# Softplus taken from ScalarE's own table, in layer 0 and in the attention's exponentials

## The chip, the cores and the metric

The kernel runs on one core of one Trainium2 chip. The metric is device time in microseconds for one execution: lower is better. One core has a matrix engine (PE, with its weight loads shown apart as PEld), a vector engine (DVE), a scalar engine that evaluates activation functions (ACT), a general engine (POOL, hardly used here), and the queue that issues most DMA transfers (SP). Each engine runs its own instructions strictly in the order in which the program lists them, and waits for the others by semaphores.

## The reference

Three stages, one after the other, on 4 x 576 = 2304 tokens of width 512 (8 heads of 64):

```python
# 1. attention with a window of 64 positions
scores = scale * q @ k^T                      # scale = 1/8
scores = where(0 <= i - j < 64, scores, -1e9)
scores = scores - max(scores)
attn   = exp(scores); attn = attn / (sum(attn) + 1e-9)
x      = attn @ v                             # back to 2304 x 512
# 2. layer 0: 512 -> 2048 -> 512, activation softplus
h = x @ w_in
g = maximum(h, 0) + log1p(exp(-abs(h)))
x = g @ w_out
# 3. layer 1: the same shapes, activation: h >= 1: h; h <= -1: 0; else (h + 1)^2 / 4
```

All arrays are float32.

## The kernel before

**Layers.** Each layer goes over five blocks of tokens (four of 512 and one of 256). Within a block, a step takes one slice of 128 of the 2048 hidden units (two slices in the block of 256 tokens): `g1` makes the hidden values `h` of the slice in a PSUM bank (there are two such banks), then the activation is made by ACT and DVE, and two steps later (`LAG = 2`) `g2` multiplies it by the second weight matrix and adds it up in four PSUM banks `y`. The PE's order in a step is thus: the products for `h` of this step, then the products for `y` of the step two before.

**Precision.** Most products are made in a reduced format from two parts of each operand, a high part and the rest (`xh`, `xl`; `wh`, `wl`; `gh`, `gl`), as three matmuls for one product. Only the second product of layer 0's first block takes whole float32 operands (`g`, `wo`); the page counts each of those matmuls as two.

**The first block** of layer 0 is special, since everything starts there: its first four slices are worked on in two halves of 256 tokens, so that products can start as soon as the first half's attention is done. The later slices take all 512 tokens at once. While it runs, the weights arrive: each slice comes as two transfers of 512 KB (`raw`, three buffers, from the tensor shown as in_w), and each is decoded by one ACT operation (line 123) and three DVE operations (lines 124 to 126) into `bits` (the first matrix) or `wo` (the second). `halves` then makes `wh` (ACT, line 133) and `wl` (DVE, line 134). For `bits` that is needed at once; for `wo` the parts are needed from the second block on, and the queue of DVE has them wherever the scheduler put them.

**The attention** goes in units of 128 tokens, each of four parts: twice `sub_scores` (for the heads' even and odd halves), `sub_transpose` and `sub_pv`. Scores (PE, line 220) are copied (ACT), masked and their maximum taken (DVE, lines 251 to 253), exponentials made with their sums (ACT, line 257, four operations of 64 columns each time), divided (DVE, lines 261 to 263); the result `p` is transposed (PE, line 273), masked out of PSUM (DVE, line 286, into `pt`), multiplied by v (PE, line 305) and split into `xh` and `xl` (ACT line 312, DVE line 315). The attention of a block is spread over the steps of the block before it.

**The order** of all instructions on each engine is settled when the program is built: a scheduler with priorities places them by its own estimates, and the hardware then keeps that order.

**Layer 0's activation before** is the function `softplus`: ACT makes |h| out of PSUM, then exp(-|h|) = e, then (in the first block) u = 1 + e, and log(u); DVE makes u in the other blocks, then u - 1 - e, subtracts it from the logarithm as a correction, and adds max(h, 0), again out of PSUM. From the second block on, the helper `parts` then makes `gh` (ACT) and `gl` (DVE). Layer 1's `quadratic` uses `parts` as well and is not touched.

Of the kernel before, what the change touches and what calls it, by code (L numbers as in the profile page):

```python
# [1 line left out]

# [6 lines left out]
F32 = mybir.dt.float32  # L9
F32R = mybir.dt.float32r  # L10
I32 = mybir.dt.int32
AF = mybir.ActivationFunctionType
ALU = mybir.AluOpType
# [4 lines left out]
P = 128  # L18
# [4 lines left out]
NF = DFF // P  # L23
SCALE = 1.0 / D ** 0.5
MASKED = -1e9 / SCALE
EPS = 1e-9
LAG = 2
AHEAD = 1

# [10 lines left out]
def tile_window_attention_two_ffn(  # L40
# [10 lines left out]
    V, A, T = nc.vector, nc.scalar, nc.tensor  # L51
# [5 lines left out]
    gpool = ctx.enter_context(tc.tile_pool(name="g", bufs=3))  # L57
    tpool = ctx.enter_context(tc.tile_pool(name="tmp", bufs=2))
# [1 line left out]
    psum = ctx.enter_context(tc.tile_pool(name="psum", bufs=1, space=bass.MemoryType.PSUM))  # L60
    dpool = ctx.enter_context(tc.tile_pool(name="dram", bufs=1, space=bass.MemoryType.DRAM))

    A.preload_act_table_set("natural_log_exp_and_others")


    ident = cpool.tile([P, P], F32, name="ident")
# [27 lines left out]
    def pt(tag):  # L94
        return psum.tile([P, 512], F32, tag=tag, name=tag, bufs={"y": 4, "h": 2, "a": 2}[tag])
# [55 lines left out]
    sub_dve = {}  # L151
# [59 lines left out]
    def score_products(dbl, bank):  # L211
        banks = [pt(bank).rearrange("p (a s j) -> p a s j", a=2, s=2) for _ in range(2)]
        for s in range(2):
            qt, kt = qks.pop(2 * dbl + s)
            lo = 0 if (2 * dbl + s) % NCB else CB
            for a2 in range(2):
                for par in range(2):
                    for u in range(2):
                        a, r, o = 2 * a2 + par, slice(u * CB, (u + 1) * CB), slice(par * CB, (par + 1) * CB)
                        T.matmul(banks[u][o, a2, s, lo:], qt[r, a, r], kt[r, a, -(2 * CB - lo):],  # L220
                                 start=True, stop=True)
        return banks
# [3 lines left out]
    def sub_scores(dbl, u, bank):  # L226
        if u == 0:
            p2s[dbl] = apool.tile([P, NP, 2, CB], F32, tag="p2", name="p2")
        pr = p2s[dbl][:, 2 * u:2 * u + 2]
        sel = pr.rearrange("p a s j -> p (a s) j")  # L230
        mx = apool.tile([P, NP], F32, tag="mx", name="mx")
        sm = apool.tile([P, NP], F32, tag="sm", name="sm")

        def pe():
            if u == 0:
                scs[dbl] = score_products(dbl, bank)

        def a1():
            sc = scs[dbl][u]
            first = [s for s in range(2) if (2 * dbl + s) % NCB == 0]  # L240
            for s in first:
                V.memset(pr[:, :, s, :], MASKED)
            if first:
                s = 1 - first[0]
                A.copy(pr[:, :, s, :], sc[:, :, s, 0:CB])
            else:
                A.copy(pr, sc[:, :, :, 0:CB])

        def d1():
            sc = scs[dbl][u].rearrange("p a s j -> p (a s) j")  # L250
            V.copy_predicated(sel, msel.rearrange("p (o j) -> p o j", o=1).to_broadcast([P, NP, CB]), sc[:, :, CB:])
            V.tensor_reduce(mx, sel, axis=AX.X, op=ALU.max)
            sub_dve[dbl, u] = V.tensor_scalar_mul(mx, mx, -SCALE).ins  # L253

        def a2():
            for i in range(NP):
                A.activation(sel[:, i, :], sel[:, i, :], AF.Exp, bias=mx[:, i:i + 1], scale=SCALE,  # L257
                             accum_out=sm[:, i:i + 1])

        def d2():  # L260
            V.tensor_scalar_add(sm, sm, EPS)
            V.reciprocal(sm, sm)
            V.tensor_tensor(sel, sel, sm.rearrange("p (a o) -> p a o", o=1).to_broadcast([P, NP, CB]), op=ALU.mult)

        return pe, a1, d1, a2, d2

    def sub_transpose(dbl, bank):
# [102 lines left out]
    def parts(e, n):  # L370
        gh = gpool.tile([P, 512], F32R, tag="gh", name="gh")[:, :n]
        gl = gpool.tile([P, 512], F32R, tag="gl", name="gl")[:, :n]
        A.copy(gh, e)  # L373
        V.tensor_tensor(gl, e, gh.bitcast(F32), op=ALU.subtract)  # L374
        return gh, gl

    def softplus(h, n, split):

        e = tpool.tile([P, 512], F32, tag="e", name="e")[:, :n]
        u = tpool.tile([P, 512], F32, tag="u", name="u", bufs=1)[:, :n]  # L380
        l = tpool.tile([P, 512], F32, tag="l", name="l", bufs=1)[:, :n]
        g = e if split else gpool.tile([P, 512], F32, tag="gl", name="g")[:, :n]
        A.activation(e, h, AF.Abs)
        A.activation(e, e, AF.Exp, scale=-1.0)
        if not split:
            A.activation(u, e, AF.Copy, bias=1.0)
        else:
            V.tensor_scalar_add(u, e, 1.0)
        A.activation(l, u, AF.Ln)
        V.scalar_tensor_tensor(e, u, 1.0, e, op0=ALU.subtract, op1=ALU.subtract)  # L390
        V.tensor_tensor(l, l, e, op=ALU.subtract)  # L391
        V.scalar_tensor_tensor(g, h, 0.0, l, op0=ALU.max, op1=ALU.add)  # L392
        return parts(g, n) if split else (g,)

    def quadratic(h, n, split):

# [79 lines left out]
    for layer, i, f, kf, c0, n in steps:  # L476
# [33 lines left out]
        h = pt("h")[:, :kf * n]  # L510
        for j in range(kf):
            g1(layer, f + j, c0, n, *xs[layer, i], h[:, j * n:(j + 1) * n])
        if len(pend) >= LAG:
            emit_g2(pend.pop(0))
        g = (softplus, quadratic)[layer](h, kf * n, (layer, i) != (0, 0))
        pend.append((layer, i, f, kf, c0, n, g))
    while pend:
# [38 lines left out]
```

## Time and profile before

| | before |
|---|---|
| time, median of 3 runs | 908.78 us (906.93 to 909.26) |
| the profiled execution: its own time | 910.36 us |
| the profiled execution: span of the trace | 908.6 us |
| PE busy | 876.2 us (96% of the span) |
| PEld busy | 713.6 us (79%) |
| DVE busy | 621.7 us (68%) |
| ACT busy | 425.8 us (47%) |
| mean granted clock of TensorE | 0.996 of full speed |

The span is what the trace covers, from the first to the last instruction; the execution's own time is some 1.7 us more. Busy shares are means over the whole span; matmuls are pipelined and their ends are modelled, so that a busy PE may still have short holes. Times in the rows below are microseconds from the start of the span unless they say ns.

### The profile page before, as it was taken

Reading aid. Unit: us, or ns where it says so; the run is one execution under the profiler, and the core shown is the slowest. Engines: PE = TensorE matmul, PEld = TensorE weight load, DVE = VectorE, ACT = ScalarE, POOL = GpSimd, SP = SyncE. Lnnn points to the kernel's source line nnn. Section 1 sums busy time; section 2 is a strip of 40 time slices with the busy share of each in tenths; the row PEclk is TensorE's granted clock in tenths of the full one; section 3 lists DMA queues with packets and bytes.
Section 4 is the critical chain, followed back from the end, with each engine's and each line's share of the span. In section 5 each row is a group of like instructions: output and inputs, shape, how many; then the busy total and the mean of one; then the engine's idle time right before and its main releaser. Section 6 shows DMA issues by size and latency. Waiting matters only on the chain.

```text
span 908.6 us, 13022 instructions
## 1 busy us (share of the span) xinstructions
PE 876.2 (96%) x4984; PEld 713.6 (79%) x4984; DVE 621.7 (68%) x1166; ACT 425.8 (47%) x958; POOL 1.5 (0%) x10
## 2 busy tenths in 40 slices
PE   3889999899999999999999999999999999999998
PEld 2677656699888888888888888888888888888897
DVE  5899899797777787777999799854335333533342
ACT  5577684555455555554766455432223222322221
POOL 0000000000000000000000000000000000000000
PEclk9999999999999999999999999999999999999999
DMA  8474642334211231200632254120002000200010
GB/s 282 164 217 144 226 155 70 117 82 117 81 41 54 71 116 48 70 1 28 211 110 93 83 195 147 62 93 0 1 1 94 1 0 1 70 1 0 1 48 23
DMA packets 45374, 75.42 MB, mean 83 GB/s; under 512 B 4864, under 2 KB 21760, under 8 KB 45312
## 3 DMA queue, kind: packets, MB, share of 16 engines
q1 hardware_dynamic: 42912, 70.01, 23.9%
q10 hardware_dynamic: 2400, 4.59, 1.4%
q8 instruction: 39, 0.64, 0.3%
q14 instruction: 23, 0.19, 0.1%
HBM read 65.14 MB, written 9.44 MB: 82 GB/s over the span
## 4 chain that ended last, share of the span: by engine, by line
PE 83%; DVE 8%; DMA 3%; ACT 3%; issue 2%; SPq 0%; ACTq 0%; DVEq 0%
PE h L345 40%; PE y L365 22%; PE y L357 17%; DMA raw<-in_w 3%; PE a L305 2%; PE a L220 2%; DVE wl L134 1%; ACT p L257 1%; DVE pt L286 1%; PE a L273 1%; DVE l L391 1%; DVE e L390 1%; DVE wo L126 1%; DVE bits L125 1%; DVE g L392 1%
## 5 line engine op out<-in xcount | busy, mean ns | idle before, releaser
L345 PE MATMUL h<-xh,wh 128*128 128x512 f32 (+1 forms) x656 | 246.7, 376 | 4.5 <-DVE g L392 1.6
L345 PE MATMUL h<-xl,wh 128*128 128x512 f32 (+1 forms) x656 | 240.8, 367 | 0.5 <-DVE xl L315 0.3
L345 PE MATMUL h<-xh,wl 128*128 128x512 f32 (+1 forms) x656 | 240.6, 367 | 0.1
L345 PEld LDWEIGHTS h<-xh,wh 128*128 128x128 f32 x656 | 125.2, 191 | 30.0 <-ACT wh L133 3.7
L345 PEld LDWEIGHTS h<-xh,wl 128*128 128x128 f32 x656 | 125.3, 191 | 20.6 <-issue 0.3
L345 PEld LDWEIGHTS h<-xl,wh 128*128 128x128 f32 x656 | 125.2, 191 | 20.4 <-DVE xl L315 0.9
L373 ACT CAST gh<-e 128x512 fp32r<-128x512 f32 x128 | 79.4, 620 | 115.9 <-DVE e L392 68.5
L399 ACT ACTIVATE e<-e 128x512 f32<-128x512 f32 x72 | 45.5, 632 | 187.0 <-DVE e L398 186.9
L374 DVE TENSOR_TENSOR gl<-e,gh 128x512 fp32r<-128x512 f32 x128 | 88.3, 690 | 55.2 <-ACT gh L373 53.2
L398 DVE TENSOR_SCALAR e<-h 128x512 f32<-128x512 f32 x72 | 49.7, 690 | 104.1 <-PE h L345 104.1
L365 PE MATMUL y<-wh,gh 128*128 128x512 f32 x288 | 112.1, 389 | 0.0
L365 PE MATMUL y<-wl,gh 128*128 128x512 f32 x288 | 112.1, 389 | 0.0
L365 PE MATMUL y<-wh,gl 128*128 128x512 f32 x288 | 112.0, 389 | 0.0
L357 PE MATMUL y<-gh,wl 128*128 128x512 f32 (+1 forms) x256 | 93.2, 364 | 0.0
L357 PE MATMUL y<-gl,wh 128*128 128x512 f32 (+1 forms) x256 | 92.8, 362 | 0.0
L357 PE MATMUL y<-gh,wh 128*128 128x512 f32 (+1 forms) x256 | 92.8, 362 | 0.0
L400 DVE TENSOR_TENSOR e<-h,e 128x512 f32<-128x512 f32 x72 | 49.7, 690 | 41.0 <-ACT e L399 40.5
L365 PEld LDWEIGHTS y<-wh,gl 128*128 128x128 f32 x288 | 54.0, 188 | 11.3
L365 PEld LDWEIGHTS y<-wh,gh 128*128 128x128 f32 x288 | 54.1, 188 | 11.1
L365 PEld LDWEIGHTS y<-wl,gh 128*128 128x128 f32 x288 | 54.1, 188 | 10.8
L357 PE MATMUL y<-g,wo 128*128 128x512 f32 (+1 forms) x160 | 59.5, 514 | 0.0
L257 ACT ACTIVATE p<-p,mx 128x64 f32<-128x64 f32 x144 | 48.2, 336 | 23.7 <-DVE mx L253 23.6
(78 smaller groups left out, 1076.3 us busy)
## 6 DMA issues: line engine op xcount, KB each, us to landing
raw<-in_w SPq DMA_DIRECT2D x64, 512.0 KB, 3.9
qt<-in_q SPq DMA_DIRECT2D x34, 256.0 KB, 3.9
vt<-in_v SPq DMA_DIRECT2D x31, 256.0 KB, 2.9
kt<-in_k SPq DMA_DIRECT2D x29, 256.0 KB, 4.0
vt<-x2d SPq DMA_DIRECT2D x16, 256.0 KB, 5.4
x2d<-o SPq DMA_DIRECT2D x5, 512.0 KB, 2.9
out<-o SPq DMA_DIRECT2D x5, 512.0 KB, 3.1
x2d<-o ACTq DMA_DIRECT2D x4, 512.0 KB, 4.7
```

The source lines that it names most:

```text
L125: V.scalar_tensor_tensor(t, hi, -2 ** 31, t, op0=ALU.bitwise_and, op1=ALU.bitwise_or)
L220: T.matmul(banks[u][o, a2, s, lo:], qt[r, a, r], kt[r, a, -(2 * CB - lo):], start=True, stop=True)
L257: A.activation(sel[:, i, :], sel[:, i, :], AF.Exp, bias=mx[:, i:i + 1], scale=SCALE, accum_out=sm[:, i:i + 1])
L305: T.matmul(po[hf * CB:(hf + 1) * CB, a, s, :], vts[s][r, hd:hd + D], pp[s][r, 2 * hf + a // 2, a % 2, :], start=True, stop=True)
L345: T.matmul(h, w, x, start=i == 0, stop=i == len(ops) - 1)
L357: T.matmul(y[m][:, c0:c0 + n], w, x, start=f + i + c0 == 0, stop=f == NF - 1 and i == len(ops) - 1)
L365: T.matmul(y[t], l, r, start=f == 0 and i == 0, stop=f == NF - 1 and i == 2)
L373: A.copy(gh, e)
L374: V.tensor_tensor(gl, e, gh.bitcast(F32), op=ALU.subtract)
L398: V.tensor_scalar(e, h, -1.0, 1.0, op0=ALU.max, op1=ALU.min)
L399: A.activation(e, e, AF.Square, bias=0.5, scale=0.5)
L400: V.tensor_tensor(e, h, e, op=ALU.max)
```

## The change

Layer 0's activation is made by ACT's function Softplus, straight from the PSUM bank. In the first block, one ACT operation writes `g`, and DVE has nothing to do. In the other blocks, ACT evaluates Softplus twice from the same bank, once into `gh` (the reduced format) and once into `e` (float32), and DVE subtracts the two to get `gl`.

The attention's exponentials use the same function, so that one activation table serves the whole kernel: for a very negative argument softplus(t) is nearly exp(t), so softplus(s - 18) is nearly exp(s) times a constant, which the division by the sum cancels. The 18 goes into the bias (line 253's operation takes a second scalar), and the 1e-9 of the division is scaled to match. The number and shapes of these operations stay as they are.

```diff
--- before.py
+++ after.py
@@ -1,3 +1,4 @@
+import math
 from contextlib import ExitStack
 
 import concourse.bass as bass
@@ -23,7 +24,9 @@
 NF = DFF // P
 SCALE = 1.0 / D ** 0.5
 MASKED = -1e9 / SCALE
-EPS = 1e-9
+
+DOWN = 18.0
+EPS = 1e-9 * math.exp(-DOWN)
 LAG = 2
 AHEAD = 1
 
@@ -60,7 +63,7 @@
     psum = ctx.enter_context(tc.tile_pool(name="psum", bufs=1, space=bass.MemoryType.PSUM))
     dpool = ctx.enter_context(tc.tile_pool(name="dram", bufs=1, space=bass.MemoryType.DRAM))
 
-    A.preload_act_table_set("natural_log_exp_and_others")
+    A.preload_act_table_set("softplus")
 
 
     ident = cpool.tile([P, P], F32, name="ident")
@@ -250,11 +253,11 @@
             sc = scs[dbl][u].rearrange("p a s j -> p (a s) j")
             V.copy_predicated(sel, msel.rearrange("p (o j) -> p o j", o=1).to_broadcast([P, NP, CB]), sc[:, :, CB:])
             V.tensor_reduce(mx, sel, axis=AX.X, op=ALU.max)
-            sub_dve[dbl, u] = V.tensor_scalar_mul(mx, mx, -SCALE).ins
+            sub_dve[dbl, u] = V.tensor_scalar(mx, mx, -SCALE, -DOWN, op0=ALU.mult, op1=ALU.add).ins
 
         def a2():
             for i in range(NP):
-                A.activation(sel[:, i, :], sel[:, i, :], AF.Exp, bias=mx[:, i:i + 1], scale=SCALE,
+                A.activation(sel[:, i, :], sel[:, i, :], AF.Softplus, bias=mx[:, i:i + 1], scale=SCALE,
                              accum_out=sm[:, i:i + 1])
 
         def d2():
@@ -376,21 +379,17 @@
 
     def softplus(h, n, split):
 
+        if not split:
+            g = gpool.tile([P, 512], F32, tag="gl", name="g")[:, :n]
+            A.activation(g, h, AF.Softplus)
+            return (g,)
         e = tpool.tile([P, 512], F32, tag="e", name="e")[:, :n]
-        u = tpool.tile([P, 512], F32, tag="u", name="u", bufs=1)[:, :n]
-        l = tpool.tile([P, 512], F32, tag="l", name="l", bufs=1)[:, :n]
-        g = e if split else gpool.tile([P, 512], F32, tag="gl", name="g")[:, :n]
-        A.activation(e, h, AF.Abs)
-        A.activation(e, e, AF.Exp, scale=-1.0)
-        if not split:
-            A.activation(u, e, AF.Copy, bias=1.0)
-        else:
-            V.tensor_scalar_add(u, e, 1.0)
-        A.activation(l, u, AF.Ln)
-        V.scalar_tensor_tensor(e, u, 1.0, e, op0=ALU.subtract, op1=ALU.subtract)
-        V.tensor_tensor(l, l, e, op=ALU.subtract)
-        V.scalar_tensor_tensor(g, h, 0.0, l, op0=ALU.max, op1=ALU.add)
-        return parts(g, n) if split else (g,)
+        gh = gpool.tile([P, 512], F32R, tag="gh", name="gh")[:, :n]
+        gl = gpool.tile([P, 512], F32R, tag="gl", name="gl")[:, :n]
+        A.activation(gh, h, AF.Softplus)
+        A.activation(e, h, AF.Softplus)
+        V.tensor_tensor(gl, e, gh.bitcast(F32), op=ALU.subtract)
+        return gh, gl
 
     def quadratic(h, n, split):
 
```

Counted over the built programs, ACT goes from 826 to 654 instructions as the order lists them and DVE from 1168 to 884, PE keeps its 4330, and both versions have one ACT_TABLE_LOAD, at the start. Since the scheduler places instructions by its own estimates, the order changes too, in the first third of the program. Lines of the changed program stand three lower up to the activation (line 133 becomes 136).

**First place: ACT, about 31 us into the trace of before**, from the attention's exponentials `p_296` on (`g` is the activation, `h` its PSUM bank). Before:

```order
L257 ACTIVATE p_296,sm<-p_296,mx 128x64 x8
L383 ACTIVATE e<-h 128x256
L133 CAST wh_1542<-wo 128x512
L384 ACTIVATE e<-e 128x256
L123 ACTIVATE wo<-raw 128x512
L386 ACTIVATE u<-e 128x256
L133 CAST wh_450<-bits 128x512
L389 ACTIVATE l<-u 128x256
L383 ACTIVATE e<-h 128x256
L123 ACTIVATE bits<-raw 128x512
```

The changed program, from the same operation on:

```order
L260 ACTIVATE p_296,sm<-p_296,mx 128x64 x8
L384 ACTIVATE g<-h 128x256
L136 CAST wh_1362<-wo 128x512
L126 ACTIVATE wo<-raw 128x512
L136 CAST wh_441<-bits 128x512
L384 ACTIVATE g<-h 128x256
L126 ACTIVATE bits<-raw 128x512
L384 ACTIVATE g<-h 128x256
L126 ACTIVATE wo<-raw 128x512
L315 CAST xh<-a 128x4x128
L136 CAST wh_1435<-wo 128x512
```

Where the first activation took four operations with other work between them, it takes one, and two more activations and the next decodes (lines 123 and 126 of the two programs) have moved up behind it.

**Second place: DVE, at the border of the first and the second block**, about 152 us into the trace of before: the splits of `wo` (line 134, now 137) and the maximum of the scores `p_1485`, in the changed program `p_1305`. Before:

```order
L315 TENSOR_TENSOR xl<-a,xh 128x4x128
L134 TENSOR_TENSOR wl_1969<-wo,wh_1968 128x512
L134 TENSOR_TENSOR wl_1973<-wo,wh_1972 128x512
L134 TENSOR_TENSOR wl_2074<-wo,wh_2073 128x512
L134 TENSOR_TENSOR wl_2078<-wo,wh_2077 128x512
L134 TENSOR_TENSOR wl_2200<-wo,wh_2199 128x512
L390 SCALAR_TENSOR_TENSOR e<-u,e 128x512
L134 TENSOR_TENSOR wl_2204<-wo,wh_2203 128x512
L391 TENSOR_TENSOR l<-l,e 128x512
L134 TENSOR_TENSOR wl_2304<-wo,wh_2303 128x512
L392 SCALAR_TENSOR_TENSOR g<-h,l 128x512
L251 COPY_PREDICATED p_1485<-msel,a 128x256 x2
```

The changed program, up to the same operation (`pt` is the masked transpose of the unit before):

```order
L289 TENSOR_TENSOR pt_1185<-a,mown 64x512
L289 TENSOR_TENSOR pt_1185<-a,mprev 64x512
L289 TENSOR_TENSOR pt_1186<-a,mown 64x512
L289 TENSOR_TENSOR pt_1186<-a,mprev 64x512
L137 TENSOR_TENSOR wl_1972<-wo,wh_1971 128x512
L137 TENSOR_TENSOR wl_1976<-wo,wh_1975 128x512
L318 TENSOR_TENSOR xl<-a,xh 128x4x128
L137 TENSOR_TENSOR wl_2068<-wo,wh_2067 128x512
L254 COPY_PREDICATED p_1305<-msel,a 128x256 x2
```

Between `xl` and the masked copy of the scores stood seven splits and three operations of the activation; now one split stands there.

## Rows read from the trace of the kernel before

**Rows 1.** The page, busy tenths of PE in 40 equal slices.

```profile
PE   3889999899999999999999999999999999999998
```

**Rows 2.** Busy time by stretch: length, then PE, PEld, DVE, ACT, POOL (instructions), clock, DMA.

```profile
37.75:74.31 36.56, 30.50 (x258) 25.15 (x257) 33.50 (x84) 25.38 (x81) 0.00 (x0) 0.95 0.60 187
74.31:152.83 78.52, 77.16 (x376) 49.17 (x375) 73.38 (x135) 55.62 (x109) 0.00 (x0) 1.00 0.43 142
152.83:174.15 21.32, 17.82 (x137) 12.37 (x133) 18.11 (x38) 9.21 (x28) 0.00 (x0) 0.92 0.30 97
174.15:250.00 75.85, 75.30 (x699) 67.98 (x700) 59.63 (x130) 41.69 (x128) 0.00 (x0) 1.00 0.36 106
250.00:425.00 175.00, 175.00 (x1128) 142.03 (x1128) 133.23 (x260) 93.77 (x242) 0.00 (x0) 1.00 0.17 52
425.00:908.60 483.60, 479.40 (x2204) 400.27 (x2202) 278.82 (x454) 180.79 (x302) 0.00 (x0) 1.00 0.18 59
```

**Rows 3.** Waits of PE, 31.5 to 74.4 us: total us, times, longest.

```profile
PE a L305 <- DVE pt L286: 2.4, 2, 1.8
PE h L345 <- DVE g L392: 1.6, 2, 0.9
PE h L345 <- ACT wh L133: 0.9, 1, 0.9
```

**Rows 4.** Waits of PE, 74.4 to 250 us, the same columns.

```profile
PE a L273 <- DVE p L263: 3.9, 3, 2.6
PE h L345 <- DVE sm L262: 1.3, 1, 1.3
```

**Rows 5.** Timeline of PE, single rows: start, us, instruction [idle before].

```profile
60.79 0.28 PE L345 MATMUL h<-xh,wh 128*128 128x256 f32 x1
60.91 0.28 PE L345 MATMUL h<-xl,wh 128*128 128x256 f32 x1
...
68.41 1.89 PE L357 MATMUL y<-g,wo 128*128 128x256 f32 x8
...
155.81 3.60 PE L357 MATMUL y<-g,wo 128*128 128x512 f32 x8
```

**Rows 6.** Timeline of PE, the attention's three kinds of products.

```profile
58.06 0.69 PE L305 MATMUL a<-pt,vt 128*64 128x64 f32 x16 [0.57 <-DVE pt L286]
...
61.95 0.89 PE L220 MATMUL a<-kt,qt 64*64 64x128 f32 x16
...
161.99 0.41 PE L273 MATMUL a<-ident,p 128*128 128x128 f32 x2 [2.58 <-DVE p L263]
```

**Rows 7.** Two stretches of half clock, columns as in rows 2.

```profile
41.50:45.00 3.50, 3.50 (x27) 2.53 (x28) 2.59 (x5) 0.46 (x1) 0.00 (x0) 0.51 0.24 80
...
164.40:167.80 3.40, 3.40 (x28) 3.17 (x28) 3.31 (x6) 0.68 (x2) 0.00 (x0) 0.51 0.00 0
```

**Rows 8.** Groups of ACT and DVE by shape: busy us, mean ns | idle before.

```profile
L384 ACT ACTIVATE e<-e 128x512 f32<-128x512 f32 x68 | 42.8, 630 | 1.5
L383 ACT ACTIVATE e<-h 128x512 f32<-128x512 f32 x68 | 40.2, 591 | 21.6 <-PE h L345 21.3 <-ACT wh L133 0.3
L390 DVE SCALAR_TENSOR_TENSOR e<-u,e 128x512 f32<-128x512 f32 x68 | 47.0, 690 | 2.4 <-ACT u L386 0.8
L63 ACT ACT_TABLE_LOAD x1 | 1.3, 1283 | 0.8 <-PEq L546 0.8
```

**Rows 9.** Timelines of ACT and DVE, the softmax of two attention units.

```profile
159.53 0.35 ACT L257 ACTIVATE p<-p,mx 128x64 f32<-128x64 f32 x1 [5.93 <-DVE mx L253]
...
175.35 0.64 ACT L247 COPY p<-a 128x256 f32<-128x256 f32 x2
...
179.61 0.43 DVE L263 TENSOR_TENSOR p<-p,sm 128x256 f32<-128x256 f32 x1
180.93 0.43 DVE L263 TENSOR_TENSOR p<-p,sm 128x256 f32<-128x256 f32 x1
```

**Rows 10.** The chain in order of time, 60 to 165 us: start, us, what.

```profile
69.89 4.27 DMA raw<-in_w
```

## The prediction

> **What bounds the kernel now.** I read the page's slices first: PE is at 9 tenths nearly everywhere, and the low digits stand in the first five slices of 22.7 us [rows 1]. Then the busy times by stretch, cut where the blocks begin. From 250 us on PE leaves nothing: 175.00 of 175.00 us, and after 425 us only the last store's 4 us [rows 2]. There DVE has 133 and ACT 94 of 175 us of work; making that less buys nothing, since neither ends a wait of PE. Layer 1, most of that last stretch, isn't touched by the change at all. So the result is decided before 250 us, and the most that can be won there is what PE doesn't get done: 36.56 - 30.50 = 6.1 us idle in the first block's halves (37.75 to 74.31), 1.4 in its whole slices (to 152.83), 3.5 at the border to the second block (to 174.15), 0.6 after it (to 250), and what the two stretches of half clock cost [rows 2, 7]. Before 37.75 us PE waits for the first loads and the first attention, where no activation is made yet.
>
> Who is late there? The waits of PE name DVE nearly every time: the masked transposes `pt` 2.4 us, the activation `g` that holds an `h` bank 1.6 us, ACT's `wh` 0.9 us [rows 3]; later the softmax result `p` 3.9 us, and 1.3 us for an `h` bank [rows 4] (the row says `sm`, but that is a neighbour in DVE's queue of the operation that releases the bank, line 392). DVE is busy 33.5 of 36.6 us and 73.4 of 78.5 us in these stretches [rows 2]. It is the engine that is late, by its queue and not by one long operation.
>
> **The change, part by part.**
>
> *The activation of the first block.* ACT loses three of four operations and DVE all three. In the halves a DVE operation of 256 columns is about 0.35 us of queue and one of 512 columns 0.6 (0.690 us with its tail [rows 8]). Over the seven halves left in 37.75 to 74.31, DVE is relieved of 7 x 3 x 0.35 = 7.4 of 33.5 us. What PE could reach there at most: 72 products for `h` at 0.12 (60.91 - 60.79), 24 for `y` at a quarter of 1.72 (the eight of a row, which are four products, take 1.89 with 0.17 of tail) [rows 5], and the attention's 4 groups at 0.6 for v, 4 at 0.9 for scores, 4 pairs at 0.3 for transposes, tails off [rows 6]. That is 8.6 + 10.3 + 2.4 + 3.6 + 1.2 = 26.1, against 36.6: 10.4 us are the upper bound, the lower one is nothing. Of it I take the whole wait for `g` (1.6: the bank is now free after one ACT operation), 1.8 of the 2.4 for `pt` and 0.6 of the 0.9 for `wh` [rows 3], and the half clock at 41.5, whose 3.5 us hold 1.75 us of work at full speed [rows 7]: it follows PE's longest hole, 1.8 us [rows 3]. Shorter breaks, whose cost hides in modelled tails, give 0.75. Sum 6.5. The attention's chain of softmax, transposes and masking stays, with nearly four fifths of DVE's queue still around it, so I don't take the rest.
>
> *The whole slices.* PE is filled but for one wait of 1.3 us for an `h` bank [rows 4]. It ends with the long activation, so I take 1.3; between nothing and 1.4.
>
> *The border.* The softmax of the first unit there starts late: ACT waits 5.93 us for `mx` [rows 9], because seven splits and three activation operations stand before it in DVE's queue. PE then waits for `p`, 2.6 us and twice more shortly [rows 4, 6], and runs at half clock from 164.4 on for 3.4 us [rows 7], which costs 1.7. In the changed order one split stands there. The unit after it shows what the softmax takes when nothing is ahead: from the copies at 175.35 to 180.04 for the first `p` and 181.36 for the second, 4.7 and 6.0 us [rows 9]. PE has work for 24 x 0.12 + 3.43 = 6.3 us between scores and transposes in the changed order (the eight at 155.81 take 3.60 with the tail [rows 5]). So the cover holds, barely; I take 3.5 of the wait and 1.5 of the clock, 5.0 in all. Without the cover up to 2 come back; bounds 0 and 5.6.
>
> *Second block.* 0.6 us idle [rows 2]; I take 0.2.
>
> *The later blocks.* ACT goes from four operations to two and DVE from five to one a step. PE is full, so nothing.
>
> *Softplus itself.* No row has it. The nearest are Exp at 0.630 us and the one that reads PSUM at 0.591 [rows 8]; below, nothing cheaper than 0.591 is seen on 512 columns, above I know no row. I take 0.6, so that the exponentials cost what they did. The Trainium skill (ScalarE: Activation LUTs, Step-by-step) says that an activation costs one element per cycle and lane whatever the function; from its 186 ns + 0.833 ns a column, 612 ns would be an estimate. The two rows lie on either side of that, so the trace agrees for the functions in it.
>
> *The moved decodes and their loads.* ACT's queue now has the decodes further ahead of the activations, so an activation can stand behind a transfer that hasn't landed. One takes 4.27 us from its issue [rows 10], and three buffers turn over. With DVE's queue shorter a buffer comes free some 2 us after its landing, 7 to 7.5 us a turn and 2.4 a transfer; a whole slice needs two per 2.72 + 3.43 = 6.2 us. And PE asks for the bank only two steps later, 9 us on. I put no cost on it.
>
> **Sum.** 6.5 + 1.3 + 5.0 + 0.2 = 13.0 us. The profiled execution took 910.36, so 897.4 by its own time; it lies 1.6 above the median of the runs, so 895.8 beside 908.8: I say **896**.
>
> **The rivals.**
>
> *A: landings hold the activations.* The chain from 60 to 165 us does go through `raw` transfers [rows 10]. For it: ACT's order above. Against: they are on that chain because DVE frees buffers late. Then the halves give 3 instead of 6.5, and 899.5 results.
>
> *B: the border's stall stays*, because DVE reaches `mx` late anyway: 5.0 less, 901. Against it: DVE has lost three of some ten operations a slice before it. A and B together: 904.5.
>
> *C: nothing for PE.* The queue's waits are only passed on to the attention's chain, whose length hasn't changed. Then within 2 us of 908. Against it: the waits for the `h` bank have no such second cause.
>
> *D: slower, by a dear Softplus.* In 250 to 425 us a step is 6.2 us, so 28 steps; ACT's four operations a step are 28 x 2.47 = 69 of its 93.8 us, `parts` counted at 0.62 [rows 2, 8], and 24.6 are left. With two of price p, ACT is full at 24.6 + 56 p = 175, p = 2.7 us, over four times Exp. At five times, 3.15, a step takes 0.88 + 6.3 = 7.2 and the 56 long steps lose about 56 us: 950. Five times isn't near any row.
>
> *E: table switches.* ACT would load a table between Softplus and the casts or the squares, 1283 ns each [rows 8], two a step. In the whole slices ACT would then have 55.6 - 12 x 3 x 0.63 + 24 x 1.28 = 64 of 78.5 us, so PE would still be fed, but the bank comes later and the border's cover goes: about 904. The built program has one load only. The Trainium skill (ScalarE: Activation LUTs, Table sets) speaks for this rival, since it says that functions come in named sets and each switch costs some 2.7 us with a drain, and names no set with Softplus.
>
> **How the numbers follow.** Forecast 0.58 (892 to 899 by the bounds of the border and of the halves); A 0.14; B 0.08; A and B 0.04; C 0.06; D 0.04; E 0.03; more than forecast, toward the bounds 10.4 and 5.6, 0.03 (891). From 891 to 902 lie the forecast, A, B and the last, 0.83, a little of it outside: 0.8. A run differs by about 0.3% from another, 2.7 us, which is what a measurement can tell: A, B, both and E are still faster by more than that, so faster 0.90, same 0.06 (C), slower 0.04 (D).
>
> **What would show it.** Right: ACT's Softplus of 512 columns near 0.6 us; one table load; no half clock at the border, PE's idle time in the halves under 3 us; the first 512-column product 6 us earlier than 74.31; DVE busy some 25 us there instead of 33.5; all steps after 250 us of unchanged length, only shifted. Wrong: PE's waits in the halves now naming ACT `g` or `raw` (A), 2 us or more before the transposes of the second block's first unit (B), Softplus over 2.7 us (D), more than one table load (E).

## The result and the profile after

The changed kernel takes 895.44 us (median of 4 runs, 894.77 to 896.29); the kernel before, run beside it, 909.02 (906.93 to 910.48). The ratio is 0.985, interval 0.983 to 0.987: 13.6 us less, where 13.0 were forecast. The page of the changed kernel, busy time and PE's slices, answers to [rows 1]:

```profile
PE 869.5 (97%) x4984; PEld 710.0 (79%) x4984; DVE 468.5 (52%) x882; ACT 326.3 (37%) x786; POOL 1.5 (0%) x10
...
PE   3989999999999999999999999999999999999998
PEclk9999999999999999999999999999999999999999
```

DVE lost 153 us of work over the span (621.7 before) and ACT 99.5 (425.8 before). The time fell by 14, because only the early stages had anything to give. To see which, both traces are cut at the same five places of PE's program: the starts of the 1st, 97th, 241st, 289th and 457th product for `h`. They part the first block's halves, its whole slices, the border (the first four slices, in two steps, of the second block, which is the one of 256 tokens), and the rest of the second block from the later blocks. Since PE makes `y` two steps late, the products for `y` of the first block's last two slices fall into the border. The busy times by these stretches, the columns as in [rows 2], first of the kernel before (all but the whole slices, which are the second line there), then of the changed kernel:

```profile
31.53:74.31 42.78, 36.58 (x283) 30.93 (x283) 38.71 (x98) 30.31 (x102) 0.00 (x0) 0.96 0.64 207
...
152.83:174.08 21.25, 17.75 (x136) 12.30 (x133) 18.04 (x37) 9.21 (x28) 0.00 (x0) 0.92 0.29 96
174.08:232.16 58.08, 57.53 (x573) 53.70 (x569) 45.99 (x105) 33.49 (x109) 0.00 (x0) 1.00 0.37 107
232.16:418.40 186.24, 186.24 (x1232) 150.92 (x1230) 142.64 (x279) 99.49 (x258) 0.00 (x0) 1.00 0.19 59
```

```profile
30.63:68.23 37.60, 33.67 (x280) 28.91 (x281) 31.90 (x78) 23.07 (x80) 0.00 (x0) 1.00 0.69 229
68.23:145.68 77.45, 77.16 (x378) 49.55 (x376) 58.30 (x105) 33.75 (x72) 0.00 (x0) 1.00 0.44 147
145.68:161.76 16.08, 15.96 (x136) 11.18 (x132) 9.97 (x22) 7.17 (x25) 0.00 (x0) 1.00 0.40 126
161.76:217.59 55.83, 55.83 (x573) 52.73 (x569) 28.95 (x74) 23.81 (x93) 0.00 (x0) 1.00 0.37 111
217.59:403.83 186.24, 186.24 (x1232) 151.00 (x1230) 71.30 (x157) 61.47 (x197) 0.00 (x0) 1.00 0.19 59
```

So the halves give 5.2, the whole slices 1.1, the border 5.2, the second block 2.25, and the later blocks, where DVE went from 142.6 to 71.3 us of work, nothing at all. All four stretches before 217.59 show the granted clock at 1.00; the two half-clock stretches of [rows 7] are gone. The first stage also starts 0.9 us earlier (30.63 against 31.53), which isn't read as an effect: over all kernels below, with either activation, this start lies between 30.1 and 31.9. With it the two traces differ by 14.8 us, 1.2 more than the medians, as the profiled execution of the kernel before lies 1.3 above its median.

PE's waits of the changed kernel, 29 to 250 us, in answer to [rows 3, 4]: total us, times, longest.

```profile
PE y L360 <- ACT g L384: 1.3, 1, 1.3
PE h L348 <- ACT xh L315: 1.0, 2, 0.7
PE a L308 <- DVE pt L289: 0.7, 1, 0.7
...
PE a L276 <- DVE sm L264: 0.5, 1, 0.5
```

The wait of 2.6 us for `p` is gone, `pt` fell from 2.4 to 0.7, and the wait for a bank that DVE held is gone. A new one leads the list, 1.3 us for the activation `g`, and it names ACT, no longer DVE. The groups of the new operations on ACT, by shape, in answer to [rows 8]:

```profile
L389 ACT ACTIVATE gh<-h 128x512 fp32r<-128x512 f32 x56 | 33.1, 591 | 104.2 <-PE h L348 101.5 <-DMA x2d<-o 2.6
L390 ACT ACTIVATE e<-h 128x512 f32<-128x512 f32 x56 | 33.0, 590 | 0.0
L384 ACT ACTIVATE g<-h 128x512 f32<-128x512 f32 x12 | 7.0, 589 | 11.8 <-PE h L348 11.8
```

Softplus of 512 columns takes 0.589 to 0.591 us, what the old operation on the same bank took (591 ns, [rows 8]). Last, the border in the changed kernel, single rows of its timeline, in answer to [rows 6, 9]:

```profile
147.79 0.35 ACT L260 ACTIVATE p<-p,mx 128x64 f32<-128x64 f32 x1 [1.34 <-DVE mx L256]
...
151.00 0.42 DVE L266 TENSOR_TENSOR p<-p,sm 128x256 f32<-128x256 f32 x1
...
152.10 0.60 PE L276 MATMUL a<-ident,p 128*128 128x128 f32 x4
```

ACT waits 1.34 us for `mx` instead of 5.93. The second `p` is ready at 151.42, and PE comes to its transposes at 152.10, after the products that cover them, without idling.

### The profile page after: what moved, and what is told of

It is laid out like the page before. It is cut to its first block, busy times and chain, and to the rows that moved or that the text cites. A ratio compares the mean times of both kernels' runs of the same rounds, so it can differ in the third digit from the quotient of the medians.

```text
span 893.8 us, 12488 instructions
## 1 busy us (share of the span) xinstructions
PE 869.5 (97%) x4984; PEld 710.0 (79%) x4984; DVE 468.5 (52%) x882; ACT 326.3 (37%) x786; POOL 1.5 (0%) x10
## 4 chain that ended last, share of the span: by engine, by line
PE 90%; DMA 5%; DVE 3%; ACT 1%; issue 1%; SPq 0%; ACTq 0%; DVEq 0%
PE h L348 42%; PE y L368 22%; PE y L360 20%; DMA raw<-in_w 5%; PE a L223 2%; PE a L308 2%; DVE pt L289 1%; PE a L276 1%; DVE wo L128 0%; DVE bits L129 0%; DVE bits L128 0%; ACT wo L126 0%; DVE wl L137 0%; ACT bits L126 0%; DVE xl L318 0%
## 5 line engine op out<-in xcount | busy, mean ns | idle before, releaser
L391 DVE TENSOR_TENSOR gl<-e,gh 128x512 fp32r<-128x512 f32 x56 | 38.7, 691 | 83.6 <-ACT e L390 82.2
L389 ACT ACTIVATE gh<-h 128x512 fp32r<-128x512 f32 x56 | 33.1, 591 | 104.2 <-PE h L348 101.5
L376 ACT CAST gh<-e 128x512 fp32r<-128x512 f32 x72 | 44.7, 621 | 47.6 <-DVE e L399 47.5
```

Of the source, the lines that this page charges most:

```text
L389: A.activation(gh, h, AF.Softplus)
```

## The experiments

The theory: the gain is DVE's queue in the first block (halves and border), and the later blocks and the price of Softplus give nothing. Its rivals: the shorter chain on ACT, the later blocks, or the attention's new exponential. All runs together, with the stage lengths of each one's profiled execution, cut as above (us; "after" is the changed kernel, and the ratio is to the kernel before, run beside it):

| kernel | median | ratio (interval) | halves | whole slices | border | second block |
|---|---|---|---|---|---|---|
| before | 909.02 | | 42.78 | 78.52 | 21.25 | 58.08 |
| after | 895.44 | 0.985 (0.983–0.987) | 37.60 | 77.45 | 16.08 | 55.83 |
| 1 long_later | 898.12 | 0.988 (0.985–0.990) | 37.85 | 76.88 | 16.01 | 58.10 |
| 2 long_first | 907.44 | 0.997 (0.996–0.999) | 42.61 | 78.83 | 20.88 | 55.83 |
| 3 exp_attention | 896.02 | 0.986 (0.983–0.988) | 36.13 | 78.09 | 16.21 | 55.96 |
| 4 splits_later | 905.48 | 0.996 (0.994–0.997) | 43.43 | 78.65 | 16.50 | 57.61 |
| 5 softplus_thrice | 895.17 | 0.985 (0.983–0.987) | 37.06 | 76.88 | 16.13 | 55.89 |
| 6 act_long | 895.60 | 0.985 (0.982–0.987) | 38.75 | 76.88 | 16.12 | 55.83 |
| 7 dve_long | 902.82 | 0.993 (0.991–0.995) | 39.80 | 77.36 | 22.11 | 55.82 |
| 8 dve_beside | 898.29 | 0.988 (0.986–0.991) | 36.82 | 77.28 | 19.85 | 55.83 |
| 9 early10 | 892.56 | 0.980 (0.978–0.982) | 40.61 | 74.02 | 14.56 | 55.83 |
| 10 early4 | 889.42 | 0.977 (0.975–0.979) | 40.43 | 69.71 | 14.55 | 55.83 |
| 11 before_early10 | 905.90 | 0.995 (0.993–0.997) | 42.86 | 78.93 | 12.32 | 62.04 |
| 12 g_first | 889.04 | 0.976 (0.975–0.978) | 41.08 | 69.71 | 14.57 | 55.83 |

Two things limit all of them. An edit also changes the order in which the scheduler issues everything around it: between kernels whose work in the halves is as good as the same (after, 1, 3 and 5), that stage differs by 1.7 us (36.1 to 37.9), so less than that in the halves is not read as an effect. And the kernel before, run beside each group of kernels, had medians of 909.0 to 910.5, so less than some 1.5 us between rows of different groups is not read either.

**1 and 2: which blocks?** The first gives the later blocks their long activation back (with copies and additions standing in for the functions), the second the first block only.

```diff
...
-        A.activation(gh, h, AF.Softplus)
...
         A.activation(e, h, AF.Softplus)
-        V.tensor_tensor(gl, e, gh.bitcast(F32), op=ALU.subtract)
-        return gh, gl
+        A.activation(e, e, AF.Copy)
+        V.tensor_scalar_add(u, e, 0.0)
+        A.activation(l, u, AF.Copy)
+        V.scalar_tensor_tensor(e, u, 0.0, e, op0=ALU.subtract, op1=ALU.subtract)
+        V.tensor_tensor(l, l, e, op=ALU.subtract)
+        V.scalar_tensor_tensor(e, h, 0.0, l, op0=ALU.mult, op1=ALU.add)
+        return parts(e, n)
```

> From the second block on, the activation has its old length again: four ACT and five DVE operations of the old shapes in the old places of the chain (copies stand in for exponential and logarithm, the arithmetic between them cancels, so the output is the same); the first block keeps the single Softplus. Theory (the gain comes from the first block's queues, and only 2.4 us of it from the second block): 896 to 898.5 us. Rival (the relief of ACT and DVE counts in every block): 902 us or more.

> The other half: in the first block the activation has its old length (four ACT and three DVE operations, copies standing in, same output), and the later blocks keep the two Softplus and one subtraction. Theory: the halves' 5.2 us and the whole slices' 1.1 are lost, and the border's 5.2 mostly too, since DVE is late again before it: 905 to 907 us. Rival (the border and the second block gain by the short activation of the second block itself): 901 us or less.

The first gives 898.12, 2.7 us above the changed kernel; the second 907.44, nearly all of the gain lost, a little beyond its range. The kernel with the long first block, the halves, whole slices and border by stretches, and behind them its first half-clock stretch:

```profile
31.57:74.18 42.61, 36.16 (x282) 30.55 (x283) 38.65 (x98) 30.00 (x102) 0.00 (x0) 0.96 0.64 208
74.18:153.01 78.83, 77.22 (x376) 49.19 (x374) 73.77 (x136) 55.67 (x109) 0.00 (x0) 1.00 0.44 142
153.01:173.89 20.88, 17.75 (x136) 12.44 (x132) 14.57 (x30) 7.17 (x25) 0.00 (x0) 0.92 0.31 97
...
40.60:44.00 3.40, 3.40 (x18) 2.46 (x14) 3.35 (x6) 0.93 (x2) 0.00 (x0) 0.50 0.35 82
```

These are the lengths of the kernel before, and both half-clock stretches are back (1.2 instead of 2.4 GHz). So of the 14 us some 11.5 come from twenty activations in the first block and 2.3 from the second block; the other 48 steps give nothing.

**3 and 5: the function.** The third keeps Exp in the attention (and the old bias and 1e-9 with it, not shown), so that ACT changes tables between it and Softplus; the fifth makes each Softplus three times.

```diff
-                A.activation(sel[:, i, :], sel[:, i, :], AF.Softplus, bias=mx[:, i:i + 1], scale=SCALE,
+                A.activation(sel[:, i, :], sel[:, i, :], AF.Exp, bias=mx[:, i:i + 1], scale=SCALE,
...
```

> The attention's exponentials by Exp again, layer 0's activation by Softplus: two activation tables, 55 table loads in the built program instead of one, 54 x 1.28 = 69 us more on ACT, all before 430 us. Theory (ACT has the room, but each load lengthens a softmax or the wait for a bank, and shows where those have no cover): 899 to 904 us. Rival (ACT is 37% busy, so all is hidden): 894 to 897 us. A second rival (PE waits for each of the loads): 930 us or more.

> Every Softplus of layer 0 is evaluated three times into the same tile: three ACT operations a step in the first block, six instead of two later; the output is unchanged. This is the price of a Softplus three times as dear. Theory (ACT has the room: six at 0.59 us are 3.5 of a 6.2 us step): 896 to 899 us, no change of the stretch after 250 us. Rival (ACT is near its limit, so the activation's price matters): 904 us or more.

Both come out at the time of the changed kernel, 896.02 and 895.17, so my theory for the third was wrong and its rival right, and the fifth cost even less than I had said. The table loads of the third:

```profile
L260 ACT ACT_TABLE_LOAD x27 | 34.6, 1283 | 16.6 <-DVE mx L256 16.3
L389 ACT ACT_TABLE_LOAD x20 | 25.7, 1283 | 0.3
L384 ACT ACT_TABLE_LOAD x7 | 9.0, 1283 | 0.1
```

One of them in ACT's timeline, at the border:

```profile
151.05 0.19 ACT L260 ACTIVATION_READ_ACCUMULATOR p<-p,mx 128x1 f32 x1
151.26 1.28 ACT L389 ACT_TABLE_LOAD   x1
152.55 0.60 ACT L389 ACTIVATE gh<-h 128x512 fp32r<-128x512 f32 x1
```

54 more loads are 69 us more on ACT, and no stage is longer than in the changed kernel by more than 0.7 us. In the whole slices ACT is busy 46 of 78 us with them: it has the room. So the half of the change that lets the attention and layer 0 share one table saves ACT's time and none of the kernel's.

**4: the border alone.** The kernel before, with the last eight splits of the output weights issued only behind the border's `mx`:

```diff
-                halves((0, osplit[0]), wo.pop(osplit[0]), 1)
+                with tc.issue_after(sub_dve[6, 1]) if osplit[0] >= 8 else ExitStack():
+                    halves((0, osplit[0]), wo.pop(osplit[0]), 1)
```

> The kernel before the change, old activation everywhere, with one edit: the splits of the second matrix for the last eight slices may start only after the maximum of the border's first softmax, so that they no longer stand before it in DVE's queue. Theory (that queue makes the border's stall of 3.5 us and the half clock behind it): 904 to 906 us, with no half clock near 165 us. Rival (DVE is late there whatever stands before the maximum, or the splits stall something else): 908 us or more.

905.48, as the theory has it. Its border, with the long activation of the kernel before still in place:

```profile
153.93:170.43 16.50, 16.50 (x136) 11.30 (x132) 16.14 (x35) 8.94 (x28) 0.00 (x0) 1.00 0.36 101
```

16.50 instead of 21.25, at full clock, with DVE busy 16.14 of 16.50: not how much DVE has to do there is what counts, but what stands ahead of `mx`.

**6, 7 and 8: load or chain?** In the first block the activation now is one operation on ACT. The sixth makes it a chain of four on ACT and none on DVE; the seventh one on ACT and three on DVE, in the chain; the eighth leaves the chain short and puts the three on DVE beside it, on a scratch tile. The edit of the seventh:

```diff
-            A.activation(g, h, AF.Softplus)
...
+            A.activation(e, h, AF.Softplus)
+            V.scalar_tensor_tensor(l, e, 0.0, e, op0=ALU.subtract, op1=ALU.subtract)
+            V.tensor_tensor(l, e, l, op=ALU.subtract)
+            V.scalar_tensor_tensor(g, h, 0.0, l, op0=ALU.mult, op1=ALU.add)
```

> First block alone: ACT does its four old operations (three are copies), DVE none; the later blocks as changed. Theory (DVE's queue is what is late, not the length of the activation): 896 to 899 us. Rival (the bank is held too long by the long chain, whoever makes it): 903 us or more.

> First block alone: ACT does one Softplus, DVE its three old operations behind it in the chain, the last one reading the bank as before (the arithmetic cancels); the later blocks as changed. Theory (DVE's queue): most of the gain is lost, 902 to 906 us. Rival (ACT's three operations made the lateness): 896 to 899 us.

> First block alone: one Softplus makes the activation as in the change, and DVE does three operations of the old length beside it, on a scratch tile that nobody waits for; the bank is free after the Softplus. It tells DVE's load from the length of the chain. Theory (load: the attention's and the weights' operations stand behind those three): 901 to 906 us. Rival (only the hold on the bank counts): 895 to 898 us.

ACT's long chain costs nothing (895.60), DVE's costs 7.4 (902.82), and the three operations beside the chain cost 2.9 (898.29), between what the theory and its rival gave. The stages tell where, halves and border of the seventh, then its waits:

```profile
30.21:70.01 39.80, 36.03 (x281) 30.91 (x281) 37.01 (x96) 22.64 (x78) 0.00 (x0) 0.96 0.66 212
...
147.37:169.48 22.11, 18.71 (x136) 13.19 (x133) 15.01 (x31) 7.17 (x25) 0.00 (x0) 0.85 0.28 92
```

```profile
PE a L276 <- DVE p L266: 2.7, 1, 2.7
PE h L348 <- DVE sm L264: 2.0, 1, 2.0
PE h L348 <- DVE g L389: 1.0, 2, 0.8
```

The same of the eighth:

```profile
30.16:66.98 36.82, 33.51 (x281) 28.87 (x281) 34.66 (x91) 22.80 (x78) 0.00 (x0) 1.00 0.65 213
...
144.26:164.11 19.85, 17.72 (x137) 12.36 (x133) 14.01 (x29) 7.12 (x25) 0.00 (x0) 0.91 0.33 102
```

```profile
PE a L276 <- DVE p L266: 1.2, 1, 1.2
```

In the halves load alone costs nothing: 36.82, though the three operations put 8.6 us on DVE there (34.7 us instead of 31.9 in all, since some decodes and splits moved out behind the stage). With DVE at the end of the chain they take 39.80, 2.2 more than in the changed kernel. Two things lie in it: PE's waits for an `h` bank that DVE's `g` holds, 1.0 us, and a stretch of 3.4 us at half clock (0.96 over the stage), which costs some 1.7; other waits are shorter. The wait `sm` of 2.0, at 48.7 us, isn't the chain's, as the eighth has it too, with 1.3. The sixth also has such a stretch at half clock, and 38.75. So neither share of the old chain alone makes the old length: on ACT it is +1.2, within what the stage varies by, on DVE +2.2. Both together make +5.0 (2). How they add up in the halves stays open.

At the border the load costs, in the chain or beside it: 22.11 and 19.85 instead of 16.08, `p` late again, and the half clock behind it. DVE's order shows how, and that it agrees with the fourth. Single rows of the eighth, from `xl` to the masked copy of the scores:

```profile
140.30 0.69 DVE L318 TENSOR_TENSOR xl<-a,xh 128x512 fp32r<-128x512 f32 x1
140.91 2.13 DVE L137 TENSOR_TENSOR wl<-wo,wh 128x512 fp32r<-128x512 f32 x3
...
145.97 2.13 DVE L137 TENSOR_TENSOR wl<-wo,wh 128x512 fp32r<-128x512 f32 x3
148.02 0.76 DVE L254 COPY_PREDICATED p<-msel,a 128x256 f32<-128x256 int32 x2
```

Eight splits and the three operations stand between the two again, in the seventh seven splits and three, as in the kernel before; in the changed kernel it is one split, with DVE idle for 5.1 us ahead of it. So what the load does there is to put the splits back ahead of `mx`.

**9 to 12: a faster version.** The first block's second product is a whole float32 one, 8 entries of 0.429 us a slice, where twelve reduced products take 2.72. With DVE relieved, the output weights might be split as soon as they are decoded, and the split activation used there: from slice 10 on (9) or from slice 4 on (10), and, to see whether this needs the change, from 10 on in the kernel before (11). `EARLY` is that slice's number. The buffers of the two parts get a fixed place for each slice (not shown).

```diff
-            if layer == 0 and part:
+            if layer == 0 and part and f < EARLY:
...
-            while osplit[0] < min(f + kf, NF):
+            while osplit[0] < min(f + kf, EARLY):
...
-        g = (softplus, quadratic)[layer](h, kf * n, (layer, i) != (0, 0))
+        g = (softplus, quadratic)[layer](h, kf * n, (layer, i) != (0, 0) or f >= EARLY)
```

> The changed kernel, with the output weights of slices 10 to 15 split into two reduced parts already when they are decoded, and with the split activation there, so that the first block's second product of these six slices is three reduced products (12 x 0.227 = 2.72 us a slice) instead of the whole float32 one (3.43). The operations of the splits are the same ones, only sooner; DVE gains one subtraction of 0.69 us a slice. Theory (DVE has been relieved in the whole slices: busy 58.3 of 77.5 us after the change; PE full, so each microsecond less of products is a microsecond less of time): 6 x 0.71 = 4.3 less, 890 to 892. Rival (a slice's split now lies between its decode and its product, and PE waits there): 894 to 898.

> The same for all twelve whole slices of the first block, 4 to 15. Theory: at most 12 x 0.71 = 8.5 less than the changed kernel; DVE then has 58.3 + 12 x 0.69 = 66.6 of 68.9 us, nearly full, so some of it is lost: 887 to 890, and below the kernel with six slices. Rival (DVE's queue is late again, waits for y's weights or for the activation's low part): 891 to 897, no better than with six.

> The kernel before, with the same early split of slices 10 to 15. The products are 4.3 us shorter here too. Theory (the gain of the early split exists only because the change relieved DVE): DVE, busy 73.4 of 78.5 us in the whole slices before, gets three more operations a slice, 6 x 3 x 0.6 = 10.8 us; the 4.3 are lost or more: 908 to 915. Rival (the early split has nothing to do with the change; PE's products alone decide): 904 to 906.

892.56 and 889.42, 2.9 and 6.0 us below the changed kernel; the ninth misses its range by half a microsecond, less than can be read here, the tenth is in it. The eleventh went against my theory: 905.90, as its rival had said, though not by its reason. Its whole slices and border:

```profile
72.99:151.92 78.93, 76.31 (x394) 52.89 (x392) 76.64 (x147) 55.07 (x110) 0.00 (x0) 1.00 0.43 142
151.92:164.24 12.32, 12.08 (x79) 10.66 (x77) 11.67 (x28) 7.34 (x26) 0.00 (x0) 1.00 0.29 86
164.24:226.28 62.04, 61.88 (x633) 57.13 (x633) 52.14 (x114) 35.63 (x111) 0.00 (x0) 1.00 0.37 116
```

In the whole slices, where the products for `y` of four of the six slices lie, 2.8 us shorter, nothing is won (78.93 against 78.52). DVE is busy 76.6 of 78.9 us there, which fits that part of the theory. But border and second block together take 74.36 instead of 79.33. The other two slices' products, 1.4 us shorter, are in that, and another order of the work leaves the border without its stall, as in the fourth. The theory had overlooked that the edit moves that too.

In 9 and 10 the whole slices give 3.4 and 7.7 us and the border 1.5, but the halves lose 3. The tenth kernel there, ACT's timeline, and behind it the stretches before and at its half clock:

```profile
50.02 0.64 ACT L127 ACTIVATE bits<-raw 128x512 f32<-128x512 f32 x1
52.37 0.69 ACT L127 ACTIVATE bits<-raw 128x512 f32<-128x512 f32 x1 [1.70 <-DMA raw<-in_w]
52.97 0.36 ACT L394 ACTIVATE g<-h 128x256 f32<-128x256 f32 x1
```

```profile
50.00:53.60 3.60, 0.63 (x3) 0.43 (x4) 3.05 (x9) 1.90 (x6) 0.00 (x0) 0.99 0.92 300
53.60:57.00 3.40, 3.40 (x10) 2.48 (x9) 1.21 (x2) 0.75 (x2) 0.00 (x0) 0.51 0.51 191
```

The activation stands behind a decode whose transfer is late, PE does nothing for most of 3.6 us, and then runs at half clock. The ninth has the same, with a decode that waits 2.30 us for its transfer. That is rival A of the prediction, in small; why the transfer is late there isn't shown. The twelfth writes the next slice's decodes behind the step's activation:

```diff
-            while wsplit[0] < min(layer * NF + f + kf + AHEAD, (layer + 1) * NF):
+            while wsplit[0] < min(layer * NF + f + kf + AHEAD * ((layer, f, c0) == (0, 0, 0) or layer), (layer + 1) * NF):
...
+        if (layer, i) == (0, 0):
+            while wsplit[0] < min(f + kf + AHEAD, NF):
+                split_w(*divmod(wsplit[0], NF))
+                wsplit[0] += 1
     while pend:
```

> The kernel with twelve early splits, with the decodes of the next slice's weights written behind the step's activation in the first block, instead of ahead of its products. In the kernel with twelve early splits an activation of 256 columns stood on ScalarE behind a decode that waited for its transfer, TensorE waited 2.4 us for it and then ran 3.4 us at half clock. Theory (that wait is the order of ScalarE's queue, rival A of the prediction): the halves take 37 to 38.5 us instead of 40.4, and the time is 886 to 888. Rival (the transfers are late in any order, so the wait moves to the next decode's readers, or DVE's queue takes its place): 889 to 892.

889.04, no different from the tenth. The stretches before and at the half clock of the twelfth:

```profile
48.00:56.90 8.90, 5.81 (x70) 4.78 (x70) 8.49 (x22) 4.74 (x19) 0.00 (x0) 1.00 0.70 233
56.90:67.10 10.20, 9.81 (x58) 8.99 (x53) 7.71 (x19) 5.53 (x18) 0.00 (x0) 0.50 0.67 215
```

PE's wait for `g` fell from 2.4 to 1.1 us, so the order of ACT's queue made 1.3 of it. But the idle time is now spread over the 9 us before, 5.81 busy of 8.90, and the half clock behind it lasts 10.2 us instead of 3.4: at 0.50 that costs 5 us where the other cost 1.7. The halves came out at 41.08, against 40.43. What takes this last loss away was not found. Kernels 10 and 12, some 6 us below the changed kernel, are the fastest of all.

## Why the prediction was right, step by step

The place of the gain was right, and at the border its mechanism too; in the halves the mechanism is shown only in part. That the total came so close, 13.6 beside 13.0, is in part luck: the halves gave 1.3 us less than forecast, the second block 2.05 more.

*What bounds the kernel.* Confirmed: the stages after 217.59 us give nothing, with DVE's work there halved.

*The halves.* 6.5 predicted, 5.2 measured. The pieces: the wait for the bank that DVE held (1.6) is gone, `pt` fell by 1.7, the half clock is gone. A new wait of 1.3 us for `g` came instead. DVE was relieved by 6.8 us over the stage (38.7 before, 31.9 after; 7.4 worked out). PE is still idle for 3.9 of 37.6 us, above the 3 that were named, and of the 6 us by which the first product of 512 columns was to come earlier (it does, at 68.23 instead of 74.31) 0.9 are the earlier start of the stage. The reason was stated too simply, as DVE's queue: 8 shows that more load in that queue costs nothing here, 6 and 7 that neither share of the chain alone makes the old length.

*The whole slices.* 1.3 predicted, 1.1 measured.

*The border.* 5.0 predicted, 5.2 measured, by the wait for `mx` and the half clock, as forecast; the cover held with 0.7 us to spare (151.42 to 152.10). Here it is the queue: 4 gets 4.75 of it from the order of DVE's queue alone, and in 8 the load loses 3.8 of it by that order.

*The second block.* 0.2 predicted, 2.25 measured: the one term that was sized wrongly. I took PE's idle time for all there was to win. Before, PE is busy 57.53 of 58.08 us in this stretch; after, the same 573 products take 55.83. The 84 score products alone, first before and then after:

```profile
L220 PE MATMUL a<-kt,qt 64*64 64x128 f32 x84 | 4.3, 274 | 0.0
```

```profile
L223 PE MATMUL a<-kt,qt 64*64 64x128 f32 x84 | 3.1, 274 | 0.0
```

One lasts as long as before, but they fill 1.2 us less. Most of that is PE's own order: before, the 32 products of one unit stand in two parts of 16 with products for `h` between them, and each part takes 1.02 us to the product behind it (188.12 to 189.14, 189.57 to 190.59); the 32 of a unit in one piece take 0.83 to 1.16. That time counts as busy. The second block's own activation brings this, as 1 (58.10 with the long one, all else as after, one unit in two parts again) and 2 (55.83 with the short one, behind a first block as before) show; how the scheduler comes to it isn't shown. Of the rest, 0.55 us is idle time and the other 0.5 lies in transposes and products for `y`.

*Later blocks.* Nothing predicted, nothing measured.

*Softplus itself.* 0.6 taken, 0.59 measured. The Trainium skill (ScalarE: Activation LUTs, Step-by-step) states the same rate for every function; the row agrees in that Softplus takes what the old operation took on the same bank. The 612 ns that the prediction worked out from the page's figures lie some 4% above the row.

*The moved decodes.* No cost was put on them. In the changed kernel the activation at 51.12 that PE waits 1.3 us for stands behind two decodes, of which one waited 0.54 us for its transfer; the wait names ACT `g`, the prediction's own sign for rival A, and 9 and 10 show more of it. So A's mechanism exists, at under half of its price of 3.5. Whether it is why the halves gave 5.2 and not 6.5 isn't shown: the difference lies within what this stage varies by.

*Rivals B to E.* B, the border's stall, went. C, nothing for PE, is refuted by the result. D needed 2.7 us a Softplus; three in a row, 1.8 us, cost nothing (5). E didn't come: one load was made. Its price, 904 for two loads a step, was tried in part only: with 54 more, about a third of that (76 steps, 152 loads), the kernel takes 896.02 (3), and "the bank comes later and the border's cover goes" doesn't show, with halves and border at 36.13 and 16.21. What two a step would cost stays open. The Trainium skill (ScalarE: Activation LUTs, What ACT_TABLE_LOAD costs) gives about 1283 ns for a load, which the rows show, and a drain of 1380 ns more, which they don't: the load at 151.26 starts 0.02 us after the operation ahead of it ends, and the activation behind it 0.01 us after the load.

## What to carry to other kernels

Find the stages in which the bounding engine has gaps, and price a shorter activation there only: twenty of 76 activations gave 11.5 of 14 us. Ask of an engine that is late what stands in its queue ahead of the operation that is waited for, not only how busy it is: a short order edit can then buy nearly a third of what a new algorithm does (4), and the same added load cost 3.8 us at the border and nothing in the halves (8). And an engine that shows 99% busy can still lose: compare the busy time of the same instructions in two traces.

## What the runs showed of the hardware that was not expected

- 54 loads of a table at 1283 ns, 69 us of ACT's time, cost no measurable time; ACT had the room, busy 46 of 78 us in the whole slices with them.
- The length of a stretch at half clock didn't go with the idle time ahead of it: 10.2 us at 0.50 behind 5.81 busy of 8.90 (12), 3.4 at 0.51 behind 0.63 of 3.60 (10), 6.8 at 0.50 behind 0.47 of 3.40 (9). So removing 1.3 us of a wait gained nothing in 12.
- PE's busy time for the same 573 products was 57.53 us in one order and 55.83 in another, at the same granted clock of 1.00.
